# The last four rows of a two-branch attention kernel: GpSimd rounds the high parts, and VectorE copies the turned rows out of PSUM but for the first

## The chip, the cores and the metric

The kernel runs on one core of a Trainium2 chip. The metric is the device time of one execution in microseconds; the time of a kernel is the median of its runs. A core has five engines that work side by side, each through its own instructions in their order: TensorE (PE, with its weight loads as PEld) multiplies into PSUM, VectorE (DVE) and ScalarE (ACT) read and write PSUM and SBUF, GpSimd (POOL) works on SBUF, and SyncE (SP) issues transfers. An engine waits for another by semaphores.

## The reference: what is computed

Two attention branches read one input x (2048 positions, 512 features), each with 32 heads of 16 features; a sigmoid gate mixes them.

```python
x = A_x
g = _sigmoid((x * gate_w).sum(-1, keepdims=True))
a = _A_ref(x, A_wqkv, A_wo)
b = _B_ref(x, B_wq, B_wk, B_wv, B_wo)
return g * a + (1 - g) * b
```

Branch A attends from each position to 8 positions, 2 apart, at and before it. Branch B attends from every position to all 2048, with one key and one value head shared by all 32 query heads: softmax(q k / 4) v for each head. Each branch ends in a product with its own 512 x 512 matrix wo. All inputs and the output are float32.

## The kernel before

**Parts.** TensorE's float32 products are made of rounded parts: a value is split into a high part, which is rounded to the type float32r, and a low part, the rest. A product of two such values takes three passes (high by high, high by low, low by high), and the rounding is a plain copy into a float32r tile.

**Branch B in steps.** The queries are cut into 32 units of four heads and 512 positions, the keys into 16 tiles of 128. One step, of 512 in all, is one unit with one key tile. `exp_pair` (L473) puts the scores of two heads into a two-bank PSUM tile by two products of half the array (L478), and ScalarE takes their exps (L480); that is done twice in a step, for the tiles pe_84 and pe_85 (`eb`). `weighted` (L485) then adds the values weighted by the exps of the step before into the tile po, eight products in the trace (L488). At the end of a unit VectorE turns po (L502).

**Maxima.** Ahead of its steps each unit needs the maxima of its scores. The "fills" compute scores for the maxima alone (L328), in pairs into the tile pm (`m2`) or singly into ps (`m1`), and VectorE reduces them (L348, L359). When a unit's last fill is reduced, its maxima go through GpSimd and DMA into the query tiles (L437 to L468). Fills are put between the steps where there is room. Where a unit's maxima are nearly due, `pause` (L873) puts in a pair at once, in whichever of pe_84, pe_85 and pm the planner takes to be free first.

**The order** of each engine's instructions is written by the kernel itself (a manual schedule), while it is built. A planner keeps a model of time: `clk` for TensorE, ScalarE and VectorE, `pool` for GpSimd, and `free` for the PSUM tiles. `after(engine, ready, duration)` adds an instruction to a clock. Which fill goes where, and when deferred tasks are written out, hangs on these numbers, so that a changed duration or engine can change the order of instructions that the change doesn't name.

**Rows.** The output is made in 16 rows j of 128 positions: the turned output of branch A for the row times wo_a, plus that of branch B times wo_b. The first 12 rows are made in `out_phase` (L736). The last four are made in `spread` (L784), whose products are spread over the steps, up to four items in a step (five in a row's last); an item is two products of half the array into pm (L820). A row has 21 items: nine with branch B's own parts (`own0` high, `own1` low; 384 columns, since the last unit's part of branch B is added later), then twelve with branch A's turned parts (`turned0`, `turned1`; 512 columns).

For that, `prepare` (L641) rounds the high part of branch B's columns out of the tile ob on ScalarE (L645), and GpSimd subtracts it to get the low part (L647). `turn_all` (L788) turns branch A's rows by four transposes on TensorE into ps (L791), and ScalarE copies them out of PSUM into the tile raw (L794). `parts_a` (L798) rounds raw to the high part on ScalarE (L801), and GpSimd subtracts (L803). All these tiles have one buffer each. The preparation of a row runs while the row before is multiplied: own after that row's ninth item, the transposes six items before its end, and the turned parts after its last item. At a row's end VectorE adds the two halves of pm into a tile of SBUF (L838, L839), for the last row ScalarE copies one half (L844).

For the first of the four rows `prepare`, `turn_all` and `parts_a` come ahead, two and more steps before its products, while the last unit's fills still run; the row's products wait in the planner until no fill is left (L810). `spread_some` (L847) hands out the items at the end of each step, ahead of `weighted`.

**The end.** After the last step, the last unit's po is turned, weighted and multiplied (L1183 to L1198), added to the four rows (L1202), and the rows are stored (L1203).

Of the kernel before, what the change touches and what calls it, by code (L numbers as in the profile page):

```python
# [8 lines left out]
AF = mybir.ActivationFunctionType  # L9
# [10 lines left out]
C = D // P  # L20
# [24 lines left out]
T_R, T_LAT, T_EXP, T_RED2, T_RED1, T_W, T_TTR = 0.23, 0.20, 0.92, 1.14, 0.61, 1.21, 0.66  # L45
# [3 lines left out]
def gated_mix_kernel(ctx, tc, xt, wa, wk, wq, wo_a, wo_b, out):  # L49
    nc = tc.nc  # L50
# [33 lines left out]
    clk = {"pe": 0.0, "act": 0.0, "dve": 0.0}  # L84

    def after(eng, ready, dur):
        clk[eng] = max(clk[eng], ready) + dur
        return clk[eng]
# [220 lines left out]
    hooks, pool, done = [], 0.0, set()  # L309
# [161 lines left out]
    pe, pexp, exped = [], {}, {}  # L471
# [166 lines left out]

    turned, later = {}, {}

    def prepare(j, n):  # L641
        nonlocal pool
        hi, lo = turned[j, 1] = [pe[0].tile([P, C, P], F32R, name=f"own{x}", bufs=1) for x in range(2)]
        own = ob[j // 4][:, :n, j % 4 * P:(j % 4 + 1) * P]
        nc.scalar.activation(hi[:, :n], own, AF.Copy)  # L645
        at = after("act", clk["pe"], 0.6)
        nc.gpsimd.tensor_sub(lo[:, :n], own, hi[:, :n].bitcast(F32))  # L647
        pool = max(pool, 1e3 * at) + 1300

# [24 lines left out]
    def out_items(j, n):  # L674
        items = []
        for k, m in ((1, n), (0, C)):
            for x, w in ((0, woh), (0, wol), (1, woh)):
                items += [(lambda c=c, x=x, k=k: turned[j, k][x][:, c, :], w[k][:, c, :]) for c in range(m)]
        return items
# [56 lines left out]
    def out_phase(js, n, whole_unit):  # L736
# [14 lines left out]
        def done(at):  # L751
            x, j, i = at
            if i % 4 == 3:
                run_tasks()
                run_pool()
            if x == len(js) - 1 and i == m - 5:
                ended.add(1)
            if x == 0 and i == 1:
                turn(j, 1)
            if x == 0 and i == 6:  # L760
                later.pop(j)()
            if i == 3 * n and j != js[-1]:
                prepare(js[x + 1], n)
            if i == m - 5 and j != js[-1]:
                turn(js[x + 1], 1 - x % 2)
            if i == m - 1:
                out_store(j, x % 2)
                if j != js[-1]:
                    later.pop(js[x + 1])()
# [14 lines left out]
    def spread(js, n):  # L784

        m = 3 * (C + n)

        def turn_all(j):  # L788
            bank = m1
            for c in range(C):  # L790
                nc.tensor.transpose(bank[:, c * P:(c + 1) * P], oa[c // 2][:, j, c % 2 * P:(c % 2 + 1) * P], ident)  # L791
            after("pe", 0, 0.7)
            own = p2[0].tile([P, C, P], F32, name="raw", bufs=1)
            nc.scalar.activation(own, bank.rearrange("p (c q) -> p c q", c=C), AF.Copy)  # L794
            after("act", clk["pe"] + T_LAT, 0.6)
            return own

        def parts_a(j, own):  # L798
            nonlocal pool
            hi, lo = turned[j, 0] = [pe[0].tile([P, C, P], F32R, name=f"turned{x}", bufs=1) for x in range(2)]  # L800
            nc.scalar.activation(hi, own, AF.Copy)  # L801
            at = after("act", clk["pe"], 0.6)
            nc.gpsimd.tensor_sub(lo, own, hi.bitcast(F32))  # L803
            pool = max(pool, 1e3 * at) + 1300

        prepare(js[0], n)
        yield 1.0
        parts_a(js[0], turn_all(js[0]))
        yield 3.0
        while slots or half:  # L810
            yield 1.0
        for j in js:
            nxt = j + 1 if j != js[-1] else None
            items = []
            for i in range(m):
                items = items or out_items(j, n)
                st, mv = items[i]
                for b in range(2):
                    h = slice(64 * b, 64 * b + 64)
                    nc.tensor.matmul(m2[:, b, :], st()[h], mv[h], start=(i == 0), stop=(i == m - 1))  # L820
                after("pe", 0, T_R)
                row_left[0] = m - 1 - i
                if i == 3 * n and nxt:
                    prepare(nxt, n)
                if i == m - 6 and nxt:
                    raw = turn_all(nxt)
                if i < m - 1:
                    yield 0.0
            del turned[j, 0], turned[j, 1]
            x = len(parts)  # L830
            if x < 2:
                spare.append(p2[0].tile([P, 512], F32, name="part", tag=("own", "tr8")[x], bufs=1))
            elif x == 2:
                two = p2[0].tile([P, 2, 512], F32, name="part", tag="pr", bufs=1)
                spare.extend([two[:, 0, :], two[:, 1, :]])
            parts[j] = spare[x]
            if nxt:
                nc.vector.tensor_copy(parts[j], m2[:, 1, :])  # L838
                nc.vector.tensor_add(parts[j], m2[:, 0, :], parts[j])  # L839
                parts_a(nxt, raw)  # L840
                after("dve", clk["pe"] + T_LAT, 1.4)
                yield 1.5
            else:
                nc.scalar.activation(parts[j], m2[:, 1, :], AF.Copy)  # L844
        done.add("last")
# [270 lines left out]
    for s in range(NS + 1):  # L1116
# [18 lines left out]
        k, n = (outs + rows) // 4 - 1, C - (outs >= NJ - 4)  # L1135
        if outs == NJ - 4:
            if NU - 3 in shaped and to_go() <= 9 and not later_rows and "last" not in done:
                later_rows.append(spread(list(range(outs, NJ)), n))
            if short > 0 and steps < 2:
                pause(short)  # L1140
        elif due or outs < NJ and s and kt == 0 and outs // NH in done and NHG * (k + 1) - 1 in shaped and (lead < LEAD or s >= 16 * (NHG * (k + 2) + 1)):
            if not due:
                prepare(outs, n)
                due.append(n)
            else:
                out_phase(list(range(outs, outs + rows)), due.pop(), kt == 1)
                outs += rows
                order = (0, "m1", 2)
        elif short > 0 and steps < 2:
            pause(short)  # L1150
# [28 lines left out]
    for x in range(2):  # L1179
        js = slice(2 * x, 2 * x + 2)  # L1180
        two = pe[0].tile([P, 2, 256], F32, name="ttl", tag="tt", bufs=2)
        tt, own = two[:, 0].rearrange("p (b d) -> p b d", d=32), two[:, 1]
# [12 lines left out]
    for x in range(2):  # L1195
# [3 lines left out]
        for t in range(2):  # L1199
            j = NJ - 4 + 2 * x + t  # L1200
# [32 lines left out]
```

## Time and profile before

| what | us |
|---|---|
| median of three runs (1491.42 to 1492.02) | 1491.83 |
| the profiled execution | 1492.03 |
| its span in the trace | 1490.3 |
| busy: TensorE, ScalarE, VectorE, GpSimd | 1476.7, 1282.2, 1193.3, 1023.9 |
| first of the changed instructions, on ScalarE (L645) | starts at 1413.58 |
| first product of the last four rows (L820) | starts at 1419.49 |
| copy of the last row's half of pm (L844) | starts at 1473.52 |
| last weighted group (L488) | starts at 1478.35 |

The page gives each engine's busy time as a share of the span. A group row has line, engine, operation, out<-in with shapes and the count, then busy us and mean ns of one, then the engine's idle us ahead of them and what ended it. A timeline row has start and length in us, then engine, line and operation, with the idle time ahead of it in brackets. A row of the chain of waits has start, length, and the engine and line that the end of the program waited for just then. A row of waits has the waiting engine and line, what it waited for, and us in total, times, longest.

### The profile page before, as it was taken

Reading aid. Unit: us, or ns where it says so; the run is one execution under the profiler, and the core shown is the slowest. Engines: PE = TensorE matmul, PEld = TensorE weight load, DVE = VectorE, ACT = ScalarE, POOL = GpSimd, SP = SyncE. Lnnn points to the kernel's source line nnn. Section 1 sums busy time; section 2 is a strip of 40 time slices with the busy share of each in tenths; the row PEclk is TensorE's granted clock in tenths of the full one; section 3 lists DMA queues with packets and bytes.
Section 4 is the critical chain, followed back from the end, with each engine's and each line's share of the span. In section 5 each row is a group of like instructions: output and inputs, shape, how many; then the busy total and the mean of one; then the engine's idle time right before and its main releaser. Section 6 shows DMA issues by size and latency. Waiting matters only on the chain.

```text
span 1490.3 us, 29441 instructions
## 1 busy us (share of the span) xinstructions
PE 1476.7 (99%) x11020; PEld 711.6 (48%) x11020; DVE 1193.3 (80%) x1817; ACT 1282.2 (86%) x1666; POOL 1023.9 (69%) x1808
## 2 busy tenths in 40 slices
PE   9999999999999999999999999999999999999998
PEld 6999889433333333333333475333333373333343
DVE  6976667788888888888888888888888888888812
ACT  5468988899999999999999988999989978989975
POOL 7876988887887988988988999788788130111020
PEclk9999999999999999999999999999999999999999
DMA  6754233021121120211211202012020000000000
GB/s 221 210 153 134 86 110 106 23 84 52 55 85 34 52 70 30 70 41 41 70 52 36 75 31 88 21 61 70 12 71 11 22 23 19 2 1 2 1 1 29
DMA packets 44343, 87.75 MB, mean 59 GB/s; under 512 B 9568, under 2 KB 26008, under 8 KB 39976
## 3 DMA queue, kind: packets, MB, share of 16 engines
q1 hardware_dynamic: 37064, 46.88, 10.3%
q0 software_dynamic: 6560, 37.95, 7.6%
q8 instruction: 86, 1.41, 0.4%
q10 hardware_dynamic: 576, 1.05, 0.2%
q14 instruction: 57, 0.47, 0.1%
HBM read 59.02 MB, written 26.30 MB: 57 GB/s over the span
## 4 chain that ended last, share of the span: by engine, by line
PE 91%; ACT 4%; POOL 2%; DVE 1%; issue 1%; DMA 0%; DVEq 0%; SPq 0%; ACTq 0%; POOLq 0%
PE po L488 34%; PE pe L478 26%; PE pm L328 8%; PE pe L1067 7%; PE ps L328 4%; PE pe L748 4%; PE pm L413 3%; PE ps L413 1%; PE pm L820 1%; PE po L413 1%; ACT pexp L480 1%; ACT dd L423 1%; POOL qraw L213 1%; POOL qlo L220 1%; PE pe L183 1%
## 5 line engine op out<-in xcount | busy, mean ns | idle before, releaser
L480 ACT ACTIVATE pexp<-pe 128x1024 f32<-128x1024 f32 x1022 | 988.1, 1022 | 101.8 <-PE pe L478 98.5
L348 DVE TENSOR_REDUCE mx<-pm 128x2 f32<-128x1024 f32 x511 | 623.7, 1220 | 145.0 <-PE pm L328 141.7
L488 PE MATMUL po<-pexp,vst 128*32 128x512 f32 x4096 | 545.6, 605 | 0.3 <-ACT pexp L480 0.3
L478 PE MATMUL pe<-qst,kst 64*128 64x512 f32 x1916 | 524.5, 455 | 1.6 <-ACT pexp L480 1.6
L478 PEld LDWEIGHTS pe<-qst,kst 64*128 64x128 f32 x1916 | 214.9, 184 | 416.0 <-ACT pexp L480 406.4
L359 DVE TENSOR_REDUCE mx<-ps 128x1 f32<-128x512 f32 x455 | 309.4, 680 | 3.6 <-PE ps L328 3.6
L328 PE MATMUL pm<-kst,qst 62*128 62x512 f32 x971 | 197.6, 399 | 0.7 <-ACT pexp L480 0.4
L548 POOL TENSOR_TENSOR pr<-aext 128x256 f32<-128x256 f32 x256 | 182.0, 737 | 1.7 <-DMA aext<-ad 1.5
L328 PE MATMUL ps<-kst,qst 62*128 62x512 f32 x429 | 180.4, 421 | 0.0
L608 POOL TENSOR_TENSOR oa<-oa,av 128x256 f32<-128x256 f32 x224 | 164.1, 733 | 15.2
L488 PEld LDWEIGHTS po<-pexp,vst 128*32 128x32 f32 x4096 | 80.8, 108 | 176.4 <-issue 166.6
L605 POOL TENSOR_TENSOR av<-aext,lg 128x256 f32<-128x256 f32 x224 | 139.4, 622 | 12.5
L328 PEld LDWEIGHTS ps<-kst,qst 62*128 62x128 f32 x429 | 78.9, 184 | 69.8 <-DVE mx L359 66.6
L1067 PE MATMUL pe<-wah,xh 64*128 64x384 f32 (+1 forms) x504 | 109.0, 339 | 0.4 <-ACT gate L253 0.4
L1067 PE MATMUL pe<-wal,xh 64*128 64x384 f32 (+1 forms) x504 | 109.4, 338 | 0.0
L1067 PE MATMUL pe<-wah,xl 64*128 64x384 f32 (+1 forms) x504 | 109.2, 337 | 0.0
L423 ACT ACTIVATE dd<-pm 128x512 f32<-128x512 f32 x164 | 91.0, 608 | 17.9 <-PE pm L413 11.9
L514 POOL TENSOR_TENSOR rl<-rl,gate_t 128x16 f32<-128x16 f32 x31 | 6.9, 221 | 144.3 <-DVE rl L508 144.1
L433 DVE CUSTOM_DVE_ANT_0 dd<-ps,dd 128x512 f32<-128x512 f32 x82 | 56.7, 692 | 54.6 <-PE ps L413 30.0
L328 PEld LDWEIGHTS pm<-kst,qst 62*128 62x128 f32 x971 | 93.8, 187 | 7.1 <-DVE mx L348 3.9
L554 POOL TENSOR_TENSOR tr<-pr 128x512 f32<-128x512 f32 x64 | 81.7, 1276 | 4.2
L554 POOL TENSOR_TENSOR tr<-tr 128x256 f32<-128x256 f32 (+1 forms) x128 | 72.4, 566 | 7.9
(214 smaller groups left out, 1903.9 us busy)
## 6 DMA issues: line engine op xcount, KB each, us to landing
aext<-ad POOLq DMA_DIRECT2D x32, 1056.0 KB, 5.4
ad<-stage SPq DMA_DIRECT2D x32, 384.0 KB
qst<-qd SPq DMA_DIRECT2D x60, 128.0 KB
xraw<-xt SPq DMA_DIRECT2D x16, 256.0 KB
qd<-qhi SPq DMA_DIRECT2D x16, 256.0 KB
qd<-qlo SPq DMA_DIRECT2D x16, 256.0 KB
qst<-qd SPq DMA_DIRECT2D x60, 64.0 KB
qst<-ml SPq DMA_DIRECT2D x212, 2.0 KB
```

The costliest lines, as they stand in the source:

```text
L328: nc.tensor.matmul(dst, qst[home(v)[0]][b:b + 62, pr, t * P:(t + 1) * P], kst[b:b + 62, kc * 512:(kc + 1) * 512], start=True, stop=True)
L348: nc.vector.tensor_reduce(m[:, :, pr, t, kc], dst, AX.X, ALU.max)
L359: nc.vector.tensor_reduce(m[:, odd, pr, t, kc:kc + 1], dst, AX.X, ALU.max)
L423: nc.scalar.activation(dd[0][:, odd], m2[:, odd, :], AF.Abs)
L478: nc.tensor.matmul(bank[:, odd, :], kst[b:b + 64, kt * P:(kt + 1) * P], qst[home(u)[0]][b:b + 64, pr, :], start=True, stop=True)
L480: nc.scalar.activation(e, bank, AF.Exp, scale=SCALE)
L488: nc.tensor.matmul(po[32 * i:32 * i + 32, :], vst[:, kt, :], pexp[s, i // 2][:, i % 2, :], start=(kt == 0), stop=(kt == NJ - 1))
L548: nc.gpsimd.tensor_mul(pr[:, k], q, e[:, o:o + NH, AC:2 * AC])
L554: nc.gpsimd.tensor_add(nx, cur[:, :, 0:n], cur[:, :, n:2 * n])
L605: nc.gpsimd.tensor_mul(av, e[:, o:o + NH, 2 * AC:].rearrange("p j (h d) -> p j h d", d=DH), lg[:, w].unsqueeze(3).to_broadcast([P, NH, AG, ...
L608: nc.gpsimd.tensor_add(ao, ao, av)
L1067: nc.tensor.matmul(front[2 if x == last else x % 2][0][:, b, :n], l[h], r[h], start=(i == 0), stop=(i == 3 * C - 1))
```

## The change

In the last four rows the high parts of own and turned are rounded by GpSimd's `tensor_copy` in place of ScalarE's activation. The raw copy out of PSUM goes from ScalarE to VectorE for the second to fourth of these rows and stays on ScalarE for the first. The first 12 rows call `prepare` as before. The planner's entries go along: the rounding no longer moves ScalarE's clock, GpSimd's clock is moved 1.3 us further, and the raw copy is entered as 0.7 us of VectorE.

```diff
-    def prepare(j, n):
+    def prepare(j, n, copy=None):
...
-        nc.scalar.activation(hi[:, :n], own, AF.Copy)
-        at = after("act", clk["pe"], 0.6)
+        if copy:
+            copy(hi[:, :n], own)
+            at = max(clk["pe"], pool / 1e3) + 1.3
+        else:
+            nc.scalar.activation(hi[:, :n], own, AF.Copy)
+            at = after("act", clk["pe"], 0.6)
         nc.gpsimd.tensor_sub(lo[:, :n], own, hi[:, :n].bitcast(F32))
         pool = max(pool, 1e3 * at) + 1300
...
             own = p2[0].tile([P, C, P], F32, name="raw", bufs=1)
-            nc.scalar.activation(own, bank.rearrange("p (c q) -> p c q", c=C), AF.Copy)
-            after("act", clk["pe"] + T_LAT, 0.6)
+            if j == js[0]:
+                nc.scalar.activation(own, bank.rearrange("p (c q) -> p c q", c=C), AF.Copy)
+                after("act", clk["pe"] + T_LAT, 0.6)
+            else:
+                nc.vector.tensor_copy(own, bank.rearrange("p (c q) -> p c q", c=C))
+                after("dve", clk["pe"] + T_LAT, 0.7)
...
-            nc.scalar.activation(hi, own, AF.Copy)
-            at = after("act", clk["pe"], 0.6)
+            nc.gpsimd.tensor_copy(hi, own)
+            at = max(clk["pe"], pool / 1e3) + 1.3
...
-        prepare(js[0], n)
+        prepare(js[0], n, nc.gpsimd.tensor_copy)
...
-                    prepare(nxt, n)
+                    prepare(nxt, n, nc.gpsimd.tensor_copy)
```

In the kernel after, the lines of `prepare` are L641 to L652, the lines behind them stand 4 to 8 further down, and L820 becomes L828.

## The prediction

> **What bounds the kernel now.** I read the page first, then the groups of the last stretch by line, then the chain of waits there, then the timeline around the two places where the chain leaves TensorE. The page names a busy TensorE and ScalarE:
>
> ```profile
> PE 1476.7 (99%) x11020; PEld 711.6 (48%) x11020; DVE 1193.3 (80%) x1817; ACT 1282.2 (86%) x1666; POOL 1023.9 (69%) x1808
> ```
>
> That is a mean over stages, and only the end of the program is touched. A step here is one key tile: four score products (L478), two exps on ScalarE (L480) and eight weighted products (L488). While the last four rows are multiplied, a step also holds eight products of L820, ten in a row's last step. The groups between 1418.9 and 1474.5 us:
>
> ```profile
> L480 ACT ACTIVATE pexp<-pe 128x1024 f32<-128x1024 f32 x41 | 39.7, 1022 | 11.8 <-PE pe L478 11.8
> ...
> L803 POOL TENSOR_TENSOR turned<-raw,turned 128x512 fp32r<-128x512 f32 x3 | 3.9, 1292 | 14.6 <-ACT turned L801 14.6
> ...
> L647 POOL TENSOR_TENSOR own<-ob,own 128x384 fp32r<-128x384 f32 x3 | 3.0, 1011 | 11.2 <-ACT own L645 11.2
> ...
> L838 DVE COPY part<-pm 128x512 f32<-128x512 f32 x3 | 2.1, 692 | 31.0 <-PE pm L820 31.0
> ...
> L801 ACT ACTIVATE turned<-raw 128x512 fp32r<-128x512 f32 x3 | 1.9, 632 | 0.0
> L794 ACT ACTIVATE raw<-ps 128x512 f32<-128x512 f32 x3 | 1.8, 605 | 0.0
> L645 ACT ACTIVATE own<-ob 128x384 fp32r<-128x384 f32 x3 | 1.6, 526 | 0.0
> ```
>
> ScalarE sat idle 11.8 us before its exps, and always for the scores of TensorE. The chain of waits, from the last fills of the maxima to the end of the rows:
>
> ```profile
> 1411.76 1.85 ACT pexp L480 x2
> 1413.60 0.39 issue
> ...
> 1415.93 0.50 ACT raw L794
> ...
> 1416.45 0.63 ACT turned L801
> 1417.08 1.83 ACT pexp L480 x2
> ...
> 1418.96 0.49 PE pe L478 x2
> ...
> 1419.49 1.20 PE pm L820 x8
> ...
> 1473.99 0.45 PE pe L478 x2
> ```
>
> From 1418.96 to 1474.44 every piece of the chain is TensorE, so in the rows proper TensorE is the bound. ScalarE carries the end only from 1411.76 to 1418.91, and there three of the copies that the change touches lie on it. A cross-check is the distance between two weighted groups, with a copy on ScalarE and without:
>
> ```profile
> 1456.78 1.07 PE L488 MATMUL po<-pexp,vst 128*32 128x512 f32 x8
> 1457.02 0.60 ACT L794 ACTIVATE raw<-ps 128x512 f32<-128x512 f32 x1
> ...
> 1459.61 1.06 PE L488 MATMUL po<-pexp,vst 128*32 128x512 f32 x8
> ...
> 1467.51 1.07 PE L488 MATMUL po<-pexp,vst 128*32 128x512 f32 x8
> ...
> 1470.10 1.06 PE L488 MATMUL po<-pexp,vst 128*32 128x512 f32 x8
> ...
> 1472.92 1.06 PE L488 MATMUL po<-pexp,vst 128*32 128x512 f32 x8
> ```
>
> A ten-product step with a copy took 1459.61 - 1456.78 = 2.83 us; in the last row, where ScalarE then has only exps, 1472.92 - 1470.10 = 2.82. An eight-product step there took 1470.10 - 1467.51 = 2.59.
>
> **The change part by part.** *ScalarE loses eleven instructions*: four of L645, four of L801, three of L794, so 4 x 0.526 + 4 x 0.632 + 3 x 0.605 = 6.4 us. Three rows' worth (3 x 1.76 = 5.3 us) lies in the stretch where ScalarE waits for TensorE: worth 0, hidden by the products. The rest is the first row's own (0.53, of which 0.39 shows in the chain) and turned (0.63), some 1.0 us of ScalarE ahead of 1418.9. Even that would have bought next to nothing, because the first row's products had to wait for VectorE as well:
>
> ```profile
> 1415.77 0.50 PE L328 MATMUL pm<-kst,qst 62*128 62x512 f32 x2
> ...
> 1416.31 1.23 DVE L348 TENSOR_REDUCE mx<-pm 128x2 f32<-128x1024 f32 x1 [1.25 <-PE pm L328]
> ...
> 1418.20 1.23 DVE L348 TENSOR_REDUCE mx<-pm 128x2 f32<-128x1024 f32 x1 [0.67 <-PE pm L328]
> ...
> 1419.48 0.53 PEld L820 LDWEIGHTS pm<-woh,own 64*128 64x128 f32 x6 [0.34 <-DVE mx L348]
> ```
>
> The reduction ends at 1419.43 and the first row's weights go in at 1419.48: the row cannot start before the last fill is reduced. So the removal alone is worth 0 to 0.05 us.
>
> *GpSimd gains eight copies.* No row shows such a copy on GpSimd; the nearest are its subtractions of the same shapes, 1.01 us and 1.29 us, and I take these (the ends: nothing, and several times as much). They are hidden:
>
> ```profile
> 1430.77 1.11 PE L820 MATMUL pm<-woh,turned 64*128 64x512 f32 x8
> ...
> 1438.91 0.86 PE L820 MATMUL pm<-woh,turned 64*128 64x512 f32 x6
> ...
> 1447.29 0.96 PE L820 MATMUL pm<-woh,own 64*128 64x512 f32 x6
> ```
>
> A row's last product ends at 1431.9 us and the next row first multiplies its turned part at 1438.91: 7.0 us for one copy. Own is released when those products begin, at about 1439, and wanted at 1447.29: 8 us. Behind the copies on GpSimd stand the subtractions, wanted later still, and small work of the last units. [...] *VectorE gains three copies* of the L838 kind, 0.69 us each: it idled 31.0 us before L838, so 0.
>
> *What moves.* The change also alters the planner's idea of when ScalarE is done, and with it the order. I compared the orders of the two built kernels: up to the first row's transposes TensorE's is the same, then it differs once. Before, the last two fills of the maxima were in two successive steps, both in bank pm, and the first row's products came in the second. After, both are in the first of these steps: the first fill goes into pe, the score bank itself, then come the scores for that bank, then the second fill in pm, then the other scores and at once the first eight products of the row. Twenty steps hold row products in both, but after they begin one step earlier, so one more plain step stands behind the rows.
>
> First term, the start of the row. TensorE is in order. The fill in pe comes at 1415.77 as now, its reduction runs 1416.31 to 1417.54 as now, but the scores for the same bank now wait for it: TensorE stands from 1416.27 to 1417.59 (0.05 us from the end of a reduction to the weights, as above). The second fill's reduction follows the scores at the distance of an ordinary step:
>
> ```profile
> 1411.16 0.50 PE L478 MATMUL pe<-qst,kst 64*128 64x512 f32 x2
> ...
> 1411.93 1.23 DVE L348 TENSOR_REDUCE mx<-pm 128x2 f32<-128x1024 f32 x1 [0.34 <-PE pm L328]
> ```
>
> That is 0.77 us: 1417.59 + 0.77 + 1.23 + 0.05 = 1419.64, so the row begins 0.16 us later than the 1419.48 of now. Below it is 0. Above, the longest wait for such a reduction in the last 160 us bounds what a hand-over may cost more:
>
> ```profile
> PEld pm L328 <- DVE mx L348: 1.7, 2, 0.8
> ```
>
> So 0 to 0.96 us, and I take 0.16, since each of its parts has a row. The 1 us that ScalarE saved is swallowed here: its copy of raw now ends at about 1416.45 - 0.39 = 1416.1, and it gets its next scores at 1418.2.
>
> Second term, the plain step at the end. The rows take as long as now. The tail before:
>
> ```profile
> 1473.92 0.74 PE L478 MATMUL pe<-qst,kst 64*128 64x512 f32 x4
> 1474.52 3.77 ACT L480 ACTIVATE pexp<-pe 128x1024 f32<-128x1024 f32 x4 [0.40 <-PE pe L478]
> ...
> 1476.52 0.50 PE L478 MATMUL pe<-qst,kst 64*128 64x512 f32 x2 [0.41 <-ACT pexp L480]
> ...
> 1476.94 1.07 PE L488 MATMUL po<-pexp,vst 128*32 128x512 f32 x8
> ...
> 1478.35 1.06 PE L488 MATMUL po<-pexp,vst 128*32 128x512 f32 x8 [0.34 <-ACT pexp L480]
> ```
>
> With one step more, its scores stand behind the weighted group of 1476.94, at 1477.95 (about 1.0 us a group in the chain). Exps follow scores by 1474.52 - 1473.92 = 0.60: 1478.55. The second exp comes (3.77 - 1.02) / 3 = 0.92 later and takes 1.02: it ends at 1480.49, and the last weighted group follows 0.06 later, as 1478.35 follows 1474.52 + 3.77: 1480.55. That is 2.20 us more. At ScalarE's pace alone it would be 2 x 0.92 = 1.83, at a row step's length 2.59; I take 2.20, because the order puts those scores behind the weighted group.
>
> Sum: 0.16 + 2.20 = **+2.36 us**, bounds 1.83 and 0.96 + 2.59 = 3.55. The profiled execution took 1492.03 us, its span 1490.3 and 1.73 around it; it becomes 1494.39. The median shown is 1491.83, 0.20 under that execution, so the forecast is 1491.83 + 2.36 = **1494.2 us**, 0.16% more.
>
> **The rivals.** *B, the freed ScalarE time counts.* If TensorE's unbroken row were only its modelled ends and ScalarE were the true bound, all 6.4 us would come off: 1491.83 - 6.4 + 2.36 = 1487.8. For it speaks ScalarE's 86%; against it the equal 2.59 us steps and the 11.8 us of ScalarE's idle time.
>
> *C, the clock drops in the new gap.* TensorE would stand idle 1.3 us at 1416.27, between busy stretches. If the granted clock fell to one half and came back after a step, that step's 2.59 us would be paid twice: 1494.2 + 2.6 = 1496.8. It decides if a gap of 1.3 us is enough to lose the clock. The only drop in the trace comes after the last product (ended at 1485.6). The rows give the window, its length, the busy time of TensorE, its weight loads, VectorE, ScalarE and GpSimd, the granted clock, and the DMA share and rate:
>
> ```profile
> 1487.00:1488.00 1.00, 0.00 (x0) 0.00 (x0) 0.00 (x0) 0.00 (x0) 0.00 (x0) 1.00 0.99 367
> 1488.00:1489.00 1.00, 0.00 (x0) 0.00 (x0) 0.00 (x0) 0.00 (x0) 0.00 (x0) 0.68 0.62 232
> ```
>
> The clock was still 1.00 after 2.4 us without a product, so 1.3 us should pass. [...]
>
> *D, GpSimd becomes late.* It decides from a copy of 7 us on, five times the subtraction of its size. At 8 us three rows would each wait 1 us: 1494.2 + 3 = 1497.2. Against it: nothing that GpSimd does here on 512 elements is above 1.3 us.
>
> **How the numbers follow.** My forecast has 80 in 100, of which 22 lie above 1494.8 (towards its upper bound) and 58 below; B has 6, C 7, D 7. What a measurement of this kernel can tell from no change is about 0.2%, 2.98 us, so "same" is 1488.85 to 1494.81. Faster 0.06 (B), same 0.58, slower 0.22 + 0.14 = 0.36. For the range the bounds, 1493.66 and 1495.38, are widened by the spread of the three runs (1491.42 to 1492.02): 1493.1 to 1496.0. B, C and D are left out, 2 in 10.
>
> **What would show it.** Right: the scores at about 1417.6 wait 1.3 us for the reduction of pe; the first product of the rows is at 1419.6; later rows' steps stay at 2.59, ten-product steps near 2.82, with ScalarE idle longer; three steps instead of two behind the rows; the last weighted group at about 1480.7. Wrong: row steps below 2.59 (B), a granted clock under 1.00 near 1417 (C), products of L820 (L828 after) that wait for GpSimd (D), or a last group within 1 us of 1478.35.

## The result, and the profile after

The changed kernel takes 1495.59 us, the median of ten runs from 1494.48 to 1497.25; the kernel before takes 1491.57 (ten runs, 1491.42 to 1492.02). The ratio is 1.0026, 95% interval 1.0018 to 1.0035: 4.0 us slower. The runs of the changed kernel scatter over 2.8 us, those of before over 0.6. The profiled execution of the changed kernel took 1496.91 us, with a span of 1495.1.

The chain of waits of the changed kernel, around the fills and the first row:

```profile
1415.31 0.46 PE pe L328 x2
...
1415.85 1.24 DVE mx L348
...
1417.13 0.50 PE pe L478 x2
1417.63 0.25 PE pm L328
...
1417.91 1.24 DVE mx L348
1419.14 0.14 issue
1419.28 2.08 PE pm L828 x8
1421.35 1.86 PE po L488 x8
1423.22 1.15 PE pe L478 x4
1424.37 1.36 PE pm L828 x7
1425.73 1.00 PE po L488 x8
```

ScalarE has left this part of the chain. Two reductions of VectorE stand in its place, first that of the fill in pe, then that of the fill in pm, and TensorE waits for both. Its own list of waits over the whole program has them, one of each:

```profile
PE pe L478 <- DVE mx L348: 1.4, 1, 1.4
...
PE pm L828 <- DVE mx L348: 1.2, 1, 1.2
```

Behind the gaps every product is slow: eight products of the row take 2.08 us where they took 1.20, a weighted group 1.86 where it took 1.00, and from 1425.73 on it takes 1.00 again. The windows show why. The columns behind the window are its length, the busy times of TensorE, weight loads, VectorE, ScalarE and GpSimd, then the granted clock (1.00 is TensorE's full speed), DMA share and rate:

```profile
1415.70:1417.10 1.40, 0.04 (x2) 0.00 (x0) 1.23 (x1) 0.00 (x0) 1.32 (x2) 1.00 0.00 0
1417.10:1418.00 0.90, 0.87 (x6) 0.48 (x6) 0.09 (x1) 0.33 (x1) 0.47 (x1) 1.00 0.00 0
1418.00:1419.20 1.20, 0.10 (x2) 0.00 (x0) 1.17 (x2) 1.20 (x2) 0.00 (x0) 0.66 0.00 0
1419.20:1421.30 2.10, 2.02 (x11) 1.27 (x11) 0.46 (x2) 0.41 (x1) 0.96 (x4) 0.50 0.00 0
...
1423.20:1424.50 1.30, 1.30 (x9) 1.10 (x8) 0.00 (x0) 0.46 (x1) 0.13 (x1) 0.50 0.07 7
1424.50:1425.70 1.20, 1.20 (x12) 0.65 (x9) 0.00 (x0) 1.20 (x2) 0.40 (x1) 0.70 0.00 0
1425.70:1428.30 2.60, 2.60 (x26) 1.21 (x26) 0.00 (x0) 1.32 (x3) 0.61 (x2) 1.00 0.00 0
```

The granted clock is 1.00 through the first gap. In the window of the second gap its mean is 0.66, so it fell to 0.50 after 0.32 x 1.20 = 0.4 us of it, at 1418.4. It came back after 0.6 x 1.2 = 0.7 us of the last but one, at 1425.2: 6.8 us at half speed.

In the rows that follow, ScalarE has less to do and waits the more. The groups of the changed kernel between 1425.7 and 1477.2 us:

```profile
L480 ACT ACTIVATE pexp<-pe 128x1024 f32<-128x1024 f32 x37 | 35.9, 1021 | 15.5 <-PE pe L478 15.5
...
L802 DVE COPY raw<-ps 128x512 f32<-128x512 f32 x3 | 2.1, 692 | 23.0 <-PE ps L795 23.0
...
L809 POOL CAST turned<-raw 128x512 fp32r<-128x512 f32 x3 | 1.8, 611 | 11.4 <-PE pm L828 11.4
L646 POOL CAST own<-ob 128x384 fp32r<-128x384 f32 x3 | 1.5, 504 | 9.1 <-PE pm L828 9.1
```

The copies on GpSimd take 0.61 and 0.50 us, half of the subtractions that I had taken for them; they wait for TensorE, not TensorE for their work. The rows end with three plain steps (steps without row products) in place of two; the last weighted group starts at 1483.27.

### The profile page after: what moved, and what is told of

It is laid out like the page before. It is cut to its first block, busy times and chain, and to the rows that moved or that the text cites. A ratio compares the mean times of both kernels' runs of the same rounds, so it can differ in the third digit from the quotient of the medians.

```text
span 1495.1 us, 29455 instructions
## 1 busy us (share of the span) xinstructions
PE 1478.5 (99%) x11020; PEld 711.5 (48%) x11020; DVE 1194.5 (80%) x1820; ACT 1277.1 (85%) x1655; POOL 1028.8 (69%) x1816
## 4 chain that ended last, share of the span: by engine, by line
PE 91%; ACT 3%; POOL 2%; DVE 2%; issue 1%; DVEq 0%; ACTq 0%; POOLq 0%
PE po L488 34%; PE pe L478 26%; PE pm L328 8%; PE pe L1075 7%; PE ps L328 4%; PE pe L752 4%; PE pm L413 2%; PE pm L828 1%; PE ps L413 1%; ACT dd L423 1%; PE po L413 1%; POOL qlo L220 1%; POOL qraw L213 1%; PE pe L183 1%; ACT pexp L480 1%
```

## The experiments

My theory after the result had three parts: the changed order costs TensorE two gaps and sends one plain step behind the rows; in some runs the clock falls in these gaps, and that makes the scatter; the new engines cost next to nothing and gain nothing. Rival 1 was that the copies on GpSimd and VectorE cost the time, rival 2 that the freed ScalarE time counts.

**engines_only: the new engines, the order of before.** The change takes its engines from after and its planner entries from before:

```diff
             copy(hi[:, :n], own)
-            at = max(clk["pe"], pool / 1e3) + 1.3
+            at = after("act", clk["pe"], 0.6)
...
-                after("dve", clk["pe"] + T_LAT, 0.7)
+                after("act", clk["pe"] + T_LAT, 0.6)
...
             nc.gpsimd.tensor_copy(hi, own)
-            at = max(clk["pe"], pool / 1e3) + 1.3
+            at = after("act", clk["pe"], 0.6)
```

> The new engines with the planner's entries of before, so TensorE's order is that of before. Theory (the lost time comes from the changed order: two gaps of TensorE, a lower clock after them, one more plain step behind the rows): 0 to +0.4 us against before, clock 1.00, the rows' steps 2.59 us, products of the first row at the same place. Rival 1 (the copies on GpSimd and VectorE are what costs): +3 us or more. Rival 2 (the freed ScalarE time counts): -1 us or better.

Measured: 1491.84 us against 1491.49, ratio 1.0002 (0.9993 to 1.0011), eleven runs from 1491.61 to 1492.30. Rival 1 falls: eleven instructions have changed engines, and nine tenths of the loss are gone. Rival 2 falls too, as nothing is gained. In the stretch from 1418.9 to 1474.5 us ScalarE's idle time ahead of its exps has grown from 11.8 to 16.7 us, close to the 5.3 us of work that left it:

```profile
L480 ACT ACTIVATE pexp<-pe 128x1024 f32<-128x1024 f32 x40 | 38.8, 1022 | 16.7 <-PE pe L478 16.7
```

**order_only: the old engines, the order of after.** The planner entries are those of after, the work is ScalarE's again:

```diff
-            nc.gpsimd.tensor_copy(hi, own)
+            nc.scalar.activation(hi, own, AF.Copy)
             at = max(clk["pe"], pool / 1e3) + 1.3
...
-                nc.vector.tensor_copy(own, bank.rearrange("p (c q) -> p c q", c=C))
+                nc.scalar.activation(own, bank.rearrange("p (c q) -> p c q", c=C), AF.Copy)
                 after("dve", clk["pe"] + T_LAT, 0.7)
...
-        prepare(js[0], n, nc.gpsimd.tensor_copy)
+        prepare(js[0], n, lambda o, i: nc.scalar.activation(o, i, AF.Copy))
```

(The other call of `prepare` is edited likewise.)

> The engines of before with the planner's entries of after, so TensorE's order is that of after. Theory: +2.4 to +5.5 us against before, varying from run to run with the granted clock, as the changed kernel does. Rival 1: within 0.3 us of before. Rival 2: the loss grows, as ScalarE has its 6.4 us back: +6 us or more in every run.

Measured: 1495.41 us against 1491.49, ratio 1.0024 (1.0016 to 1.0033), eleven runs from 1493.84 to 1496.70. The order alone makes the loss and the scatter. Four runs lie at 1493.84 to 1494.27 with a mean clock of 0.999 or 1.000, four at 1495.39 to 1495.49 and three at 1496.54 to 1496.70 with 0.997 to 0.999: three levels, some 1.5 and 1.2 us apart. (The run of 1495.39 has a mean clock of 0.999, so this figure alone does not tell the lowest level from the middle one.) The four lowest have a median of 1493.94, 2.45 us above before.

**gaps_filled: the changed kernel with TensorE kept busy in both gaps.** Products that nobody reads go into ps, whose contents ScalarE has copied by then:

```diff
+    def keep_busy(n):
+        for x in range(n):
+            nc.tensor.matmul(m1, woh[1][:, x % C, 0:P], woh[1][:, x % C, :], start=True, stop=True)
...
             fill_pair({"e0": eb[0], "e1": eb[1], "m2": m2}[key], key)
             n += 2
+            if later_rows:
+                keep_busy(5)
...
         while slots or half:
             yield 1.0
+        keep_busy(4)
         for j in js:
```

> The changed kernel with nine products without use (into ps, read by nobody) put into the two gaps of TensorE, five behind the fill in pe and four ahead of the first row. Theory: the granted clock stays at 1.00 in every run, all runs within 0.3 us of each other at +2.6 to +3.0 us against before. Rival (the clock follows something else than these gaps): the runs scatter over 2.5 us as those of the changed kernel do.

Measured: 1494.20 us against 1491.49, ratio 1.0017 (1.0009 to 1.0026), eleven runs from 1493.85 to 1494.68, the clock 0.999 or 1.000 in each. They lie within 0.8 us, not the 0.3 that I expected, but at one level. With more work on TensorE the kernel loses 2.7 us to the kernel before, where the changed one loses 4.0. The two upper levels are gone, so they come from the gaps. The waits themselves stay, filled with useless products.

**first_gap_filled and second_gap_filled.** Each has one of the two `keep_busy` calls.

> The changed kernel with five products without use behind the fill in pe, so that only the second gap of TensorE (some 1.1 us ahead of the first row) stays. Theory (the clock falls when two gaps lie in one short stretch): 1.00 in every run, +2.6 to +3.0 us against before, no scatter. Rival (one gap of over 1 us is enough): some runs at a lower clock, up to +5 us.

> The changed kernel with four products without use ahead of the first row, so that only the first gap (1.4 us, for the reduction of pe) stays. Theory: clock 1.00 in every run, +2.6 to +3.0 us against before, no scatter. Rival: some runs at a lower clock, up to +5 us.

Measured: 1494.36 us (1494.08 to 1495.54) and 1494.25 us (1494.05 to 1495.62) against 1491.56, ratios 1.0019 (1.0010 to 1.0028) for each. In 22 runs the mean clock is never below 0.999. Each kernel has one run above 1494.6 (1495.54 and 1495.62, both at 0.999), which lies at the middle level and may be a fall of the clock or not: kernels without these gaps have single runs as far out (1493.08 in before, 1493.34 in own_gpsimd below). In at least 20 of the 22 runs, then, one gap of 1.2 or 1.4 us was not enough; the two together, with 1 us of work between them, were in most runs: seven of the eleven of order_only and six of the ten of the changed kernel lie at the two upper levels. The windows of the trace of first_gap_filled show a clock that outlasts its one gap:

```profile
1418.00:1419.20 1.20, 0.01 (x2) 0.03 (x1) 1.17 (x2) 1.20 (x2) 0.00 (x0) 1.00 0.00 0
1419.20:1426.00 6.80, 6.80 (x56) 3.29 (x56) 0.38 (x2) 3.75 (x5) 4.46 (x9) 1.00 0.03 3
```

**gpsimd_only, own_gpsimd and turned_gpsimd: the small rest.** In the changed kernel and in engines_only each row's first weights go in 0.11 to 0.12 us behind the end of VectorE's last reduction or addition, where it was 0.05 to 0.06 before. Three kernels in the order of before take parts of the new engines, with the planner entries of engines_only. gpsimd_only has the raw copies back on ScalarE; own_gpsimd has in addition

```diff
-            nc.gpsimd.tensor_copy(hi, own)
+            nc.scalar.activation(hi, own, AF.Copy)
```

in `parts_a`, and turned_gpsimd in place of that calls `prepare` with ScalarE's copy.

> Order of before, the roundings on GpSimd, all raw copies on ScalarE as before. The changed kernel's later rows start some 0.1 us later behind the reduction of pm than before. Theory that the wait for GpSimd causes this: the first product of a later row again comes 0.1 us later than before, 0.2 to 0.3 us in all. Rival (it is VectorE's raw copy): row starts as before, 0 us in all.

> Order of before; only the high part of own is rounded on GpSimd. Theory (a row's first product now waits for two engines, VectorE and GpSimd, and goes in 0.09 us later, four rows): +0.3 to +0.4 us against before, distance from the end of VectorE's addition to the row's weights 0.11 us. Rival (the end of GpSimd's subtraction for turned delays it): distance 0.06 us as before, 0 us.

> Order of before; only the high part of turned is rounded on GpSimd. Theory of the double wait: 0 us against before, distance 0.06 us. Rival (the end of GpSimd's subtraction for turned delays the row): distance 0.11 us in rows two to four, +0.2 to +0.3 us.

Measured: gpsimd_only 1491.94 us against 1491.49, ratio 1.0003 (0.9993 to 1.0012); own_gpsimd 1492.02 (1491.73 to 1493.34) and turned_gpsimd 1491.68 (1491.14 to 1493.04) against 1491.56, ratios 1.0005 (0.9996 to 1.0014) and 1.0001 (0.9992 to 1.0010). The totals alone do not part these from nothing; the places do. The start of the third row and that of the fourth in own_gpsimd, in the timeline:

```profile
1447.46 0.56 PEld L828 LDWEIGHTS pm<-woh,own 64*128 64x128 f32 x6 [0.35 <-issue]
...
1460.64 0.69 DVE L847 TENSOR_TENSOR part<-pm,part 128x512 f32<-128x512 f32 x1
...
1461.11 1.29 POOL L811 TENSOR_TENSOR turned<-raw,turned 128x512 fp32r<-128x512 f32 x1 [6.77 <-ACT turned L809]
...
1461.45 0.56 PEld L828 LDWEIGHTS pm<-woh,own 64*128 64x128 f32 x6 [0.35 <-issue]
```

The fourth row of turned_gpsimd:

```profile
1459.38 1.28 POOL L811 TENSOR_TENSOR turned<-raw,turned 128x512 fp32r<-128x512 f32 x1 [0.34 <-PE pm L828]
1460.00 0.69 DVE L847 TENSOR_TENSOR part<-pm,part 128x512 f32<-128x512 f32 x1
...
1460.74 0.53 PEld L828 LDWEIGHTS pm<-woh,own 64*128 64x128 f32 x6 [0.28 <-DVE part L847]
```

And that of the kernel before:

```profile
1460.44 0.69 DVE L839 TENSOR_TENSOR part<-pm,part 128x512 f32<-128x512 f32 x1
...
1461.19 0.53 PEld L820 LDWEIGHTS pm<-woh,own 64*128 64x128 f32 x6 [0.29 <-DVE part L839]
```

From the end of VectorE's addition to the weights it is 1461.45 - 1461.33 = 0.12 us with own on GpSimd, and 1460.74 - 1460.69 = 0.05 with only turned there, as before (1461.19 - 1461.13 = 0.06). In own_gpsimd GpSimd's subtraction for turned is still running when the row starts, so the row does not wait for it. What the row has more than before is a second wait. In the trace of the changed kernel each row's first weights wait for GpSimd's semaphore, and 0.08 us ahead of them stands an instruction of TensorE of its own, 0.05 us long, that waits for VectorE's (four of them at L828). In before the weights wait for VectorE's semaphore themselves, and no such instruction is there. The distances of the others go with own too: 0.11 to 0.12 us in gpsimd_only, whose fourth row's weights go in at 1461.00 behind an addition that ends at 1460.88, and 0.05 in order_only (1461.24 - 1461.19). The raw copy is out as well, since gpsimd_only, without it on VectorE, has the same late starts (the profile names "POOL turned L811" there, which merely ended last). A row of own_gpsimd takes 1461.45 - 1447.46 = 13.99 us, where it took 1461.19 - 1447.29 = 13.90 before. The first start and three such rows give 0.06 + 3 x 0.09 = 0.33 us, of the size of the 0.35 that engines_only lost.

**tail_spread and gaps_filled_tail_spread: the plain steps.** If a plain step behind the rows costs its length because TensorE idles in it, row products belong there:

```diff
-        spread_some(4)
+        spread_some(3 if len(parts) == 3 else 4)
```

tail_spread is the kernel before with this line, gaps_filled_tail_spread is gaps_filled with it.

> The kernel before, with three items of the last row in a step in place of four, so that its products fill the plain steps at the end too. Theory (in the plain steps TensorE waits for the exps, so row products there are free while each costs 0.23 us among the others): -0.5 to -0.9 us against before. Rival (the exps of ScalarE set the end whatever TensorE does, and the products only delay the scores): 0 or slower.

> The changed kernel with both gaps filled and three items of the last row in a step, so that one plain step is left behind the rows in place of three. Theory (the step that the changed order sends behind the rows costs its length because TensorE idles there): +1.9 to +2.3 us against before, some 0.6 us less than with the gaps filled alone (+2.7). Rival: +2.7 us or more.

Measured: tail_spread 1490.76 us against 1491.71, ratio 0.9993 (0.9984 to 1.0002), its eleven runs from 1490.51 to 1491.11, all below the lowest of 21 runs of before (1491.45), though the interval of the ratio reaches over 1. Its rival falls. gaps_filled_tail_spread 1493.87 against 1491.71, ratio 1.0016 (1.0007 to 1.0025), +2.16 us where gaps_filled alone had +2.71. The intervals of these two overlap; for a gain here speaks that seven of the eleven runs lie nearer to before than any run of gaps_filled did. The runs go from 1493.43 to 1497.74, so even with both gaps filled one run came out 4 us late, and nothing here says why. In tail_spread a step of the last row is shorter by one item, as its chain shows:

```profile
1466.43 1.00 PE po L488 x8
1467.43 0.67 PE pe L478 x4
1468.09 0.70 PE pm L820 x6
1468.79 1.00 PE po L488 x8
```

A step takes 1468.79 - 1466.43 = 2.36 us, 0.23 less than with four items. No plain step is left, since row products stand in the last step too, as the timeline shows:

```profile
1474.44 0.73 PE L478 MATMUL pe<-qst,kst 64*128 64x512 f32 x4
...
1475.01 0.86 PE L820 MATMUL pm<-woh,turned 64*128 64x512 f32 x6
...
1475.80 1.07 PE L488 MATMUL po<-pexp,vst 128*32 128x512 f32 x8
...
1477.03 1.06 PE L488 MATMUL po<-pexp,vst 128*32 128x512 f32 x8 [0.16 <-ACT pexp L480]
```

This version beats both kernels, with none of the change in it.

## Why the prediction was right, and where it was not

**The bound was read rightly.** The rows are bound by TensorE, and 6.4 us less on ScalarE bought nothing: engines_only turned most of them into idle time. Rival B is refuted. (Of the three ScalarE copies that the prediction counts on the chain ahead of the rows, the raw copy of the first row stays on ScalarE; the sum takes the other two alone.)

**The order was the change that mattered,** and its two terms came out as computed, 2.45 us in the four lowest runs of order_only against the 2.36 of the sum. The timeline of order_only, whose profiled execution kept a clock of 1.00 here, has the first term:

```profile
1415.59 0.50 PE L328 MATMUL pe<-kst,qst 62*128 62x512 f32 x2
...
1417.49 0.50 PE L478 MATMUL pe<-qst,kst 64*128 64x512 f32 x2 [1.40 <-DVE mx L348]
...
1418.27 1.23 DVE L348 TENSOR_REDUCE mx<-pm 128x2 f32<-128x1024 f32 x1 [0.83 <-PE pm L328]
...
1419.55 0.53 PEld L828 LDWEIGHTS pm<-woh,own 64*128 64x128 f32 x6 [1.53 <-DVE mx L348]
```

From the first of the last two fills (here in pe) to the row's first weights it is 1419.55 - 1415.59 = 3.96 us, against 1419.48 - 1415.77 = 3.71 before: 0.25 where the sum had 0.16. The second term, the plain step, can be read from the tail of the changed kernel, where it needs 1483.27 - 1475.73 = 7.54 us from the last row's weighted group, against 1478.35 - 1472.99 = 5.36 before: 2.18 where the sum had 2.20. The row of the chain before, then those of the changed kernel:

```profile
1472.99 1.00 PE po L488 x8
```

```profile
1475.73 1.00 PE po L488 x8
...
1477.27 1.95 ACT pexp L480 x2
...
1479.26 0.49 PE pe L478 x2
1479.75 0.99 PE po L488 x8
...
1483.22 0.04 issue
1483.27 1.11 PE po L488 x8
```

In order_only, at full clock, the last weighted group starts at 1480.58, where the prediction had about 1480.7.

**Rival C happened, and my forecast had put it aside: this step failed.** I weighed a single gap of 1.3 us against the only drop in the trace, after more than 2.4 us of idle time, and found it too short. My own sum held the second gap: the row waits for a reduction from about 1418.4 to 1419.6, which stands in the first term and never came into the weighing of C. Behind the pair the clock fell to 0.50 in the profiled execution of the changed kernel, and 13 of the 21 runs with both gaps lie at the upper levels; with one such gap at least 20 of 22 runs do not lie there. The price was some 1.5 or 2.7 us (the two upper levels of order_only) where I had 2.6.

The drop in the trace before was misread too. The window from 1488 to 1489 us that the prediction shows has a mean of 0.68, and its last 0.60 us, from 1488.40 on, are at 0.50; so 0.36 us of it were at 1.00 and the clock fell at 1488.36, 2.8 us after the last product. In the changed kernel it fell at 1418.4, after a gap of 1.4 us and a part of the next, and TensorE was busy for 1.74 of the 3.41 us ahead of the fall (half as long as the 6.8 us that it lasted):

```profile
1414.97:1418.38 3.41, 1.74 (x12) 0.67 (x8) 1.70 (x2) 1.29 (x3) 1.88 (x2) 1.00 0.00 0
```

So the 2.4 us without a product that the clock outlasted in before were no measure for gaps with work between them. What share must be idle, and over what stretch, was not tried. The profiled execution of order_only is of the lowest level (1494.27 us), that of the changed kernel is among its longest (1496.91 us); what makes the middle level was not shown.

**Costed at nothing, it cost 0.3 us:** the roundings on GpSimd are hidden as work, and rival D was right to be small, but each row start got one more semaphore to wait for (an instruction of 0.05 us, and the weights 0.06 us later). I had counted when the data would be there and not the wait itself.

So the distance of 4.0 us is some 2.4 for the order, 0.3 for the double wait, and the rest, 1.3 us at the median, for the clock. The forecast of 2.36 fell short by the last two. That the range held the result is luck: it reached up to 1496.0 for a longer hand-over and a full row step, and neither came (0.25 and 2.18 us). "Same" had 0.58 of the chance and "slower" 0.36; the loss is 0.26%, slower by over the 0.2% that I had set.

## What to carry to other kernels

Where a planner writes the order, first compare the order of the built programs: here the planner's changed entries, not the changed engines, made nine tenths of the loss. Work taken off an engine that waited became waiting here (in engines_only 5.3 us less work on ScalarE, 4.9 us more idle time ahead of its exps); the free time at the end of this kernel was TensorE's, in the plain steps, and a line that moved products there gained 0.95 us. When a new gap on TensorE is weighed, add the gaps near it: two of 1.4 and 1.2 us, 1 us apart, cost up to 2.7 us here on top of their own length, where either alone mostly cost nothing more.

## What the runs showed of the hardware that was not expected

- In the changed kernel's profiled execution the granted clock fell to 0.50 with 1.4 us of idle time, 1 us of work and 0.3 to 0.4 us of idle time before it, and stayed there for 6.8 us, of which TensorE was busy for 5.9. With either gap filled, 20 of 22 runs took 1494.05 to 1494.54 us, at a mean clock of 0.999 or 1.000.
- At the end of the program the clock fell to 0.50 as well: 3.0 us after the last product in the same execution (1493.48 - 1490.44), 2.8 in before (1488.36 - 1485.60).
- In the changed kernel, engines_only, gpsimd_only and own_gpsimd the rows' first weights went in 0.11 to 0.12 us after the end of VectorE's reduction or addition, in the trace of the changed kernel with an instruction of 0.05 us ahead of them that waits for VectorE, while they wait for GpSimd; in before, order_only and turned_gpsimd they went in 0.05 to 0.06 us after it.
- GpSimd's copy from float32 to float32r took 0.61 us for 512 columns and 0.50 for 384, half of its subtraction with two inputs (1.29 and 1.01).
